# Attention and mixture-of-depths on one core: a group prepared 16 steps ahead, weights and selected rows loaded at other places in the queue

## The chip, the core and the metric

The kernel runs on one core of a Trainium2 chip. The metric is the device time of one execution in microseconds (us), where lower is better. Everything is in float32.

## The reference

Two blocks follow each other. The first is attention with normalized queries and keys, for 8 batches, 12 heads, 448 tokens and head size 64; the second routes 128 tokens of each batch through a two-layer network.

```
q_n = q / sqrt(mean(q*q) + 1e-6) * g_q           # over the head size, k_n likewise
attn = softmax(q_n @ k_n.T / sqrt(64))
x    = (attn @ v) as (8, 448, 768)
scores = x @ w_gate                               # one number per token
top    = the 128 tokens of a batch with the highest scores
out    = x, and for the tokens of top: x + sigmoid(score) * (relu(x @ w1) @ w2)
```

w1 is 768 x 1024 and w2 is 1024 x 768.

## The kernel before

**Work and its units.** The twelve heads of a batch are cut into three groups of four heads, so there are 24 groups. A group has 7 steps, one for each block of 64 keys; 168 steps in all. A step is `scores` (16 small matmuls on PE into `sc`, two exponentials of 128x448 on ACT into `p`), `values` (16 matmuls into `av`) and `add_probs` (one addition on DVE into `sum`). When the last step of a group is done, `values_out`, `sum_keys`, `invert_sums` and `to_tokens` copy, divide and transpose the result into `x`, one token per row. Three groups make a batch; `gate`, `spread`, `ranks_of`, `count` and `annotate` then find the rank of each token, `select` scatters the 128 chosen rows from `x` to DRAM (four indirect DMAs on POOL's queue), `load_selected` reads them back as `xe` on SP's queue, and `mixture` runs the two-layer network on them in pieces.

**Preparation of a group.** `prepare(n, slot)` puts six things into a table: `squares` on ACT (L193) and the reduction `sum_squares` on DVE (L199), each twice, for queries (tile 0) and keys (tile 1); the power -1/2 is on POOL (L203). Then `rows_out` (L216) writes the queries' factors to DRAM as `rows`, and `rows_in` (L228) reads them back spread over the partitions as `bc`. `scale_q` (L237, DVE) multiplies `qT` by `bc` four steps before the group's first scores. The keys' factors go into the exponential as its scale.

**Order.** The order is written by hand, and each engine executes its queue in that order. `at(slot, fn)` enters a function under a step; one pass of the main loop, here called a round, takes four steps: it emits their scores and the values of earlier ones, then runs the table's entries for its slots in two halves, and after each half a piece of the mixture, if one is running. `ready[b]` says from which round on batch b's mixture may start: the later of `now + 3` and `first_ff(b)`. All plain loads and stores are issued by SP, in order; where one has to wait for a semaphore, all behind it wait too.

Before the change, group n is prepared from step 7n - 12 on, its token tiles are loaded at 7n - 20, q at 7n - 13, k and v at 7n - 11. The first preparation of this kind, that of group 2, starts at step 4. The 14 parts of the weights (`load_w`, L181) are loaded at steps 8 to 21, with the gate's weights `wg` (L177) ahead of them. `constants` (L161 to L173), at step 9, makes a table of comparisons and the token numbers on POOL, and DVE copies the numbers to `token_f`. `load_selected` (L484) is entered three steps after the ranks' first count.

Of the kernel before, what the change touches and what calls it, by code (L numbers as in the profile page):

```python
# [10 lines left out]
F32 = mybir.dt.float32  # L11
# [6 lines left out]
def _bcast_row(ap_1d: bass.AP, parts: int) -> bass.AP:  # L18
    return dataclasses.replace(ap_1d, ap=[[0, parts]] + [list(x) for x in ap_1d.ap])
# [7 lines left out]
def fast(  # L27
# [25 lines left out]
    nc = tc.nc  # L53

    B, NP, _, S = qT.shape
    CP = 112
    NJ = S // CP
    D = 64
    NI = S // D
# [15 lines left out]
    norm_pool = ctx.enter_context(tc.tile_pool(name="norm", bufs=2))  # L75
# [65 lines left out]
    for c in range(2):  # L141
        nc.vector.memset(pick_pair[D * c : D * (c + 1), c : c + 1], 1.0)
    nc.vector.scalar_tensor_tensor(
        out=gg, in0=gcol[:, 0:1], scalar=scale, in1=gcol[:, 1:2], op0=OP.mult, op1=OP.mult
# [6 lines left out]
    wg = const.tile([CP, DM], F32, name="wg")  # L151
# [21 lines left out]
        nc.vector.tensor_copy(out=token_f, in_=token_i)  # L173

    def load_w(part):
        if part == 0:
            nc.sync.dma_start(out=wg, in_=_bcast_row(moe_w_gate, CP))  # L177
        for w, src in ((w1, moe_w1), (w2, moe_w2)):
            n = w.shape[1]
            if part < n:  # L180
                nc.sync.dma_start(  # L181
                    out=w[:, part], in_=src.rearrange("(c p) f -> p c f", p=128)[:, part]
                )
            part -= n
            if part < 0:
                return
# [3 lines left out]
    def squares(n, i):  # L190
        t = toks.pop((n, i))
        sq = norm_pool.tile([128, 2, NI, D], F32, name="sq")
        nc.scalar.activation(out=sq, in_=t, func=AF.Square, scale=scale)  # L193
        sss[n, i] = norm_pool.tile([128, 2, NI], F32, name="ss", bufs=4)
        return sq

    def sum_squares(n, i, sq):
        ss = sss.pop((n, i))
        nc.vector.tensor_reduce(out=ss, in_=sq, axis=AX.X, op=OP.add)  # L199
        nc.vector.tensor_scalar_add(out=ss, in0=ss, scalar1=1e-6)  # L200
        rinv = norm_pool.tile([128, 2, NI], F32, name="rinv", bufs=6)
        flat = "p h i -> p (h i)"
        nc.gpsimd.tensor_tensor(  # L203
            out=rinv.rearrange(flat),
            in0=ss.rearrange(flat),
            in1=neg_half.to_broadcast([128, 2 * NI]),
            op=OP.pow,
        )
        rinvs[n, i] = rinv
# [206 lines left out]
    def score_rows(b):  # L416
        t = rowss[b]
        ps = aux([128, 512], "row_ps")
        for j in range(NJ):
            nc.tensor.transpose(  # L420
                out=ps[:CP, CP * j : CP * (j + 1)], in_=t[:, j, :], identity=ident[:CP, :CP]
            )
        rows = moe_pool.tile([CP, S], F32, name="score_rows")
        nc.scalar.copy(out=rows, in_=ps[:CP, 0:S])
        rowss[b] = rows
# [153 lines left out]
    def at(slot, fn, *args):  # L579
        todo.setdefault(slot, []).append(lambda: fn(*args))  # L580
# [8 lines left out]
    def prepare(n, slot):  # L589
        sq = {}  # L590
        for i in range(2):
            at(slot + 2 * i, lambda i=i: sq.setdefault(i, squares(n, i)))
            at(slot + 2 * i + 1, lambda i=i: sum_squares(n, i, sq.pop(i)))
        at(slot + 4, rows_out, n)
        at(slot + 5, rows_in, n)

    for n in range(1, n_groups):
        s0 = NI * n
        if n > 2:
            at(s0 - 20 if n > 3 else 0, load_tok, n, 0)  # L600
            at(s0 - 20 if n > 3 else 0, load_tok, n, 1)
        at(max(s0 - 4, 3), scale_q, n)
        if n > 1:
            prepare(n, max(s0 - 12, 4))
            at(max(s0 - 13, 2), load_q, n)
            at(max(s0 - 11, 2), load_k, n)
            at(max(s0 - 11, 2), load_v, n)
    for part in range(NDC + NFC):
        at(8 + part, load_w, part)
    at(9, constants)  # L610

    def finish(n, q):

# [5 lines left out]
    now = [0]  # L619

    def last_tokens(n):
        to_tokens(n, 1)
        b, g = divmod(n, NG)
        q = now[0]

        s = PER * (q + 1) if n < n_groups - 1 else -9
        at(s, gate, n)
        if g < NG - 1:
            return
        at(s, store_x, b)  # L630
        at(s + 1, spread, b)
        task((q + 1, 1) if n < n_groups - 1 else (q + 1, 0), ranks_of, b)

    def ranks_of(b):
        score_rows(b)
        s = PER * (now[0] + 1) if b < B - 1 else -9
        at(s, count, b, (0, 1))
        at(s + 1, count, b, (2, 3))
        at(s + 2, annotate, b)
        at(s + 2, select, b)  # L640
        at(s + 3, load_selected, b)
        if b < B - 1:
            ready[b] = max(now[0] + 3, first_ff(b))
        else:
            ready[b] = 0

    def first_ff(b):


        return (units + 4 - NG * NI * (B - 2 - b)) // PER  # L650
# [15 lines left out]
    sq = {}  # L666
    sq[0, 0] = squares(0, 0)
    sum_squares(0, 0, sq.pop((0, 0)))
    sq[0, 1] = squares(0, 1)
    sum_squares(0, 1, sq.pop((0, 1)))  # L670
    sq[1, 0] = squares(1, 0)
    sq[1, 1] = squares(1, 1)
# [25 lines left out]
    moe, ready, done, q = iter(()), {}, 0, 0  # L698
# [475 lines left out]
def _build(nc, ap, cap, out):  # L1174
    D = ap["g_q"].shape[0]
    with tile.TileContext(nc) as tc:
        with tc.tile_pool(name="bound", bufs=1) as pool:
            g = pool.tile([1, 2, D], F32, name="g")
            nc.sync.dma_start(out=g[:, 0], in_=ap["g_q"].rearrange("(one d) -> one d", one=1))
            nc.sync.dma_start(out=g[:, 1], in_=ap["g_k"].rearrange("(one d) -> one d", one=1))  # L1180


            prod = pool.tile([1, D], F32, name="prod")
            nc.vector.tensor_mul(out=prod, in0=g[:, 0], in1=g[:, 1])
            nc.vector.tensor_mul(out=prod, in0=prod, in1=prod)
            top = pool.tile([1, 1], F32, name="top")
            nc.vector.tensor_reduce(out=top, in_=prod, axis=AX.X, op=OP.max)
            small = pool.tile([1, 1], I32, name="small")
            nc.vector.tensor_scalar(
                out=small,  # L1190
                in0=top,
                scalar1=MAX_SCORE * MAX_SCORE / D,
                scalar2=None,
                op0=OP.is_le,
            )
            is_small = nc.values_load(small[0:1, 0:1], min_val=0, max_val=1,
                skip_runtime_bounds_check_because="a comparison gives 0 or 1")
        with tc.If(is_small > 0) as cmp, tc.manual_schedule():  # L1198
            fast(
                tc, *(ap[n] for n in ("qT", "kT", "vp", "tok", "g2")),  # L1200
                *(ap[n] for n in _INS[5:]), cap, out,
            )
        with cmp.Else():
            general(tc, *(ap[n] for n in _INS), cap, out)
# [43 lines left out]
```

## Time and profile before

| | us |
|---|---|
| median of 3 runs (lowest, highest) | 600.18 (598.5, 601.54) |
| profiled execution | 604.69 |
| its span, first to last instruction | 603.0 |
| PE busy | 530.8 |
| DVE busy | 353.1 |
| ACT busy | 279.5 |
| POOL busy | 193.7 |

PE is TensorE, DVE VectorE, ACT ScalarE, POOL GpSimd, and SP SyncE; PEld is PE's loading of weights, SPq the issuing of DMAs on SP. A row of the timeline gives the start and the duration, the engine, the line and operation, what it writes and reads, and in brackets how long the engine had been idle and who ended that. The granted clock is the share of TensorE's 2.4 GHz that it was allowed. Line numbers are those of the kernel before.

### The profile page before, as it was taken

What the parts mean: (1) busy time and instruction counts of PE and PEld (TensorE: products, weight loads), DVE (VectorE), ACT (ScalarE), POOL (GpSimd) and SP (SyncE); (2) the same over time, 40 slices, a digit from 0 to 9 for tenths busy, and PEclk for the clock granted to TensorE, in tenths of its full rate; (3) what the DMA queues carried; (4) which work ended last, traced back from release to release, by engine and by line L of the source; (5) the groups of instructions that cost most, each with busy time, mean ns of one, the idle gap of its engine ahead of it and who ended that gap; (6) DMA issues with size and microseconds to landing.
All of it is one profiled execution on the core that took longest, in us unless ns stands there. A gap on an engine that the chain in (4) does not pass through costs nothing. (4 is left out here: it accounts for less than half of the span.)

```text
span 603.0 us, 16322 instructions
## 1 busy us (share of the span) xinstructions
PE 530.8 (88%) x7028; PEld 294.3 (49%) x7028; DVE 353.1 (59%) x699; ACT 279.5 (46%) x506; POOL 193.7 (32%) x100
## 2 busy tenths in 40 slices
PE   6793887799999799996999999999998999937995
PEld 6330323236645366442665466446643664417683
DVE  2363776966575947483557766857573856453100
ACT  3571666555645445544454546444644644511010
POOL 3352333543132623053225432535052620130200
PEclk9986988899999799997999999999999999977999
DMA  6559775765805267507534626283806521013200
GB/s 234 198 163 335 224 268 196 238 206 186 276 21 193 58 212 245 185 9 251 207 119 137 228 75 244 60 272 118 277 8 201 180 80 46 27 30 112 58 28 30
DMA packets 47108, 94.02 MB, mean 156 GB/s; under 512 B 11702, under 2 KB 29878, under 8 KB 47028
## 3 DMA queue, kind: packets, MB, share of 16 engines
q1 hardware_dynamic: 43684, 86.58, 42.8%
q0 software_dynamic: 3200, 6.31, 3.2%
q8 instruction: 57, 0.93, 0.6%
q14 instruction: 23, 0.19, 0.1%
q10 hardware_dynamic: 144, 0.00, 0.0%
HBM read 75.39 MB, written 25.36 MB: 167 GB/s over the span
## 5 line engine op out<-in xcount | busy, mean ns | idle before, releaser
L287 ACT ACTIVATE p<-sc,rinv 128x448 f32<-128x448 f32 x336 | 187.1, 638 | 123.7 <-PE sc L278 73.2
L203 POOL TENSOR_TENSOR rinv<-ss,neg_half 128x14 f32<-128x14 f32 x48 | 139.2, 2905 | 297.0 <-DVE ss L200 197.1
L278 PE MATMUL sc<-qT,kT 64*32 64x448 f32 x2688 | 164.7, 569 | 31.7 <-issue 21.5
L304 PE MATMUL av<-p,v 64*32 64x448 f32 x2688 | 160.9, 556 | 0.3 <-issue 0.2
L317 DVE TENSOR_TENSOR sum<-sum,p 128x896 f32<-128x896 f32 x120 | 130.5, 1088 | 31.7 <-ACT p L287 25.3
L278 PEld LDWEIGHTS sc<-qT,kT 64*32 64x32 f32 x2688 | 51.0, 109 | 107.2 <-issue 74.2
L304 PEld LDWEIGHTS av<-p,v 64*32 64x32 f32 x2688 | 60.9, 112 | 81.6 <-issue 74.5
L524 PE MATMUL moe_ps<-xeT,w 128*128 128x128 f32 x672 | 80.8, 278 | 0.0
L524 PEld LDWEIGHTS moe_ps<-xeT,w 128*128 128x128 f32 x672 | 78.1, 194 | 2.9 <-issue 2.9
L543 PE MATMUL moe_ps<-w,hT 128*128 128x384 f32 x224 | 77.6, 491 | 1.4 <-DVE xe L552 0.7
L373 DVE TENSOR_TENSOR x<-x_ps,rden 112x512 f32<-112x512 f32 x48 | 32.9, 688 | 44.1 <-PE x_ps L371 44.1
L199 DVE TENSOR_REDUCE ss<-sq 128x14 f32<-128x896 f32 x48 | 51.6, 1075 | 11.7 <-ACT sq L193 11.7
L543 PEld LDWEIGHTS moe_ps<-w,hT 128*128 128x128 f32 x224 | 40.5, 190 | 28.6 <-issue 2.2
L466 POOL DMA_INDIRECT selected<-x,rank x32 | 39.0, 1217 | 42.0 <-DVE x L458 34.2
L237 DVE SCALAR_TENSOR_TENSOR qT<-qT,gg,bc 128x896 f32<-128x896 f32 x23 | 26.1, 1136 | 41.7 <-DMA bc<-rows 41.7
L193 ACT ACTIVATE sq<-tok 128x896 f32<-128x896 f32 x48 | 45.6, 963 | 5.6 <-DMA tok<-in_tok_dram 5.6
L397 DVE SCALAR_TENSOR_TENSOR prod<-x,wg 112x256 f32<-112x256 f32 x96 | 40.5, 422 | 2.5
L533 ACT ACTIVATE hT<-moe_ps 128x512 f32<-128x512 f32 x14 | 8.4, 597 | 58.2 <-PE moe_ps L524 58.2
L371 PE MATMUL x_ps<-ident,xT 128*112 128x128 f32 x192 | 29.1, 281 | 3.6 <-ACT xeT L505 3.0
L561 POOL DMA_INDIRECT out_dram<-xe,row x8 | 11.0, 1374 | 61.4 <-DVE rden L359 29.5
L371 PEld LDWEIGHTS x_ps<-ident,xT 128*112 128x112 f32 x192 | 21.3, 135 | 18.1 <-issue 9.7
L317 DVE TENSOR_TENSOR sum<-p 128x896 f32<-128x896 f32 x24 | 25.8, 1076 | 6.5 <-ACT p L287 6.5
(63 smaller groups left out, 243.6 us busy)
## 6 DMA issues: line engine op xcount, KB each, us to landing
tok<-in_tok_dram SPq DMA_DIRECT2D x48, 448.0 KB, 6.9
qT<-in_qT_dram SPq DMA_DIRECT2D x24, 448.0 KB, 6.0
kT<-in_kT_dram SPq DMA_DIRECT2D x24, 448.0 KB, 7.5
v<-in_vp_dram SPq DMA_DIRECT2D x24, 448.0 KB, 7.9
out_dram<-x SPq DMA_DIRECT2D x8, 1344.0 KB, 7.1
bc<-rows SPq DMA_DIRECT2D x46, 224.0 KB, 3.8
xe<-selected SPq DMA_DIRECT2D x8, 385.0 KB, 3.2
w<-in_moe_w_dram SPq DMA_DIRECT2D x6, 512.0 KB, 10.2
```

The costliest lines, as they stand in the source:

```text
L193: nc.scalar.activation(out=sq, in_=t, func=AF.Square, scale=scale)
L199: nc.vector.tensor_reduce(out=ss, in_=sq, axis=AX.X, op=OP.add)
L203: nc.gpsimd.tensor_tensor(out=rinv.rearrange(flat), in0=ss.rearrange(flat), in1=neg_half.to_broadcast([128, 2 * NI]), op=OP.pow,)
L278: nc.tensor.matmul(out=scs[hh][o : o + 32, 0:S], lhsT=kTs[n][r, c, D * i + k0 : D * i + k0 + 32], rhs=qTs[n][r, c, :], start=True, stop=True,)
L287: nc.scalar.activation(out=p[:, hh], in_=scs[hh][:, 0:S], func=AF.Exp, scale=rinvs[n, 1][:, hh, i : i + 1],)
L304: nc.tensor.matmul(out=avs[n][c][o : o + 32, 0:S], lhsT=vs[n][r, hh, i, d0 : d0 + 32], rhs=probs[u][r, hh], start=(i == 0), stop=(i == NI ...
L317: nc.vector.tensor_tensor(out=sums[n], in0=probs[u - 1] if i == 1 else sums[n], in1=probs[u], op=OP.add)
L371: nc.tensor.transpose(out=ps[:CP, j, :], in_=t[:, j, :], identity=ident)
L397: nc.vector.scalar_tensor_tensor(out=prod, in0=xs[b][:, j, cols], scalar=1.0, in1=wg[:, cols], op0=OP.mult, op1=OP.mult, accum_out=gates[b ...
L466: w = nc.gpsimd.indirect_dma_start(out=t[:, :], out_offset=bass.IndirectOffsetOnAxis(ap=rank[:, j : j + 1], axis=0), in_=x[:, j, :], in_of ...
L524: nc.tensor.matmul(out=ps[:, 128 * i : 128 * i + n], lhsT=w1[:, dc, 128 * (f0 + i) : 128 * (f0 + i + 1)], rhs=xeT[:, dc, :n], start=(dc == 0),
L543: nc.tensor.matmul(out=ps[:n, : DM // 2], lhsT=hT[:, fc, :n], rhs=w2[:, fc, cols], start=(fc == 0), stop=(fc == NFC - 1),)
```

## The change

Groups from 2 on are prepared four steps earlier, and `rows_in` comes two steps after `rows_out` instead of one; token tiles are loaded 24 instead of 20 steps ahead. `wg` is loaded at step 7 and the weights at every second step from 18 to 44; the constants move to step 18. `load_selected` comes four steps later, except in the last batch, and a mixture may start at `now + 4`. The ring of `rinv` tiles grows from 6 to 8.

```diff
-        if part == 0:
-            nc.sync.dma_start(out=wg, in_=_bcast_row(moe_w_gate, CP))
...
-        rinv = norm_pool.tile([128, 2, NI], F32, name="rinv", bufs=6)
+        rinv = norm_pool.tile([128, 2, NI], F32, name="rinv", bufs=8)
...
         at(slot + 4, rows_out, n)
-        at(slot + 5, rows_in, n)
+        at(slot + 6, rows_in, n)
...
         if n > 2:
-            at(s0 - 20 if n > 3 else 0, load_tok, n, 0)
-            at(s0 - 20 if n > 3 else 0, load_tok, n, 1)
+            at(max(s0 - 24, 0), load_tok, n, 0)
+            at(max(s0 - 24, 0), load_tok, n, 1)
         at(max(s0 - 4, 3), scale_q, n)
         if n > 1:
-            prepare(n, max(s0 - 12, 4))
+            prepare(n, max(s0 - 16, 0))
...
     for part in range(NDC + NFC):
-        at(8 + part, load_w, part)
-    at(9, constants)
+        at(18 + 2 * part, load_w, part)
+    at(7, lambda: nc.sync.dma_start(out=wg, in_=_bcast_row(moe_w_gate, CP)))
+    at(18, constants)
...
-        at(s + 3, load_selected, b)
+        at(s + 7 if b < B - 1 else s + 3, load_selected, b)
         if b < B - 1:
-            ready[b] = max(now[0] + 3, first_ff(b))
+            ready[b] = max(now[0] + 4, first_ff(b))
```

What this does to the queues is seen best in three places. The first is SP's queue from the loads of group 2's k and v on, before (`rows` and `bc` are those of group 2):

```order
L100 DMA kT<-in_kT_dram 128x2x448
L100 DMA v<-in_vp_dram 128x896
L216 DMA rows<-rinv 64x2x7 x2
L100 DMA qT<-in_qT_dram 128x2x448
L100 DMA tok<-in_tok_dram 128x896 x2
L177 DMA wg<-in_moe_w_gate_dram 112x768
L181 DMA w_210<-in_moe_w_dram 128x1024
L228 DMA bc<-rows 64x2x448 x2
```

and after the change:

```order
L100 DMA kT<-in_kT_dram 128x2x448
L100 DMA v<-in_vp_dram 128x896
L214 DMA rows<-rinv 64x2x7 x2
L100 DMA tok<-in_tok_dram 128x896 x2
L226 DMA bc<-rows 64x2x448 x2
L608 DMA wg<-in_moe_w_gate_dram 112x768
```

Between `rows` and `bc` of group 2 there are now only two token tiles; `wg` follows `bc`, and no weight is near.

The second is SP's queue around the load of batch 2's selected rows (`xe`), before (the `rows` and the `bc` beside it are those of group 13):

```order
L100 DMA v<-in_vp_dram 128x896
L216 DMA rows<-rinv 64x2x7 x2
L484 DMA xe<-selected 128x770
L228 DMA bc<-rows 64x2x448 x2
L100 DMA qT<-in_qT_dram 128x2x448
```

and after the change (the first `bc` is that of group 13, and `rows` are those of group 14):

```order
L226 DMA bc<-rows 64x2x448 x2
L100 DMA tok<-in_tok_dram 128x896 x2
L100 DMA qT<-in_qT_dram 128x2x448
L214 DMA rows<-rinv 64x2x7 x2
L100 DMA kT<-in_kT_dram 128x2x448
L100 DMA v<-in_vp_dram 128x896
L482 DMA xe<-selected 128x770
L226 DMA bc<-rows 64x2x448 x2
```

The load has moved behind that `bc` and behind the next group's `rows`, k and v. In batch 5 it is the same, with group 21.

The third is PE's queue at the end, from the last values on, before (`den_ps` and `denT_ps` invert the last group's sums, `x_ps` are its transposes, L500 transposes `xe` of batch 6, L524 is the first layer, `row_ps` ranks batch 7):

```order
L304 MATMUL av<-p,v 32x448 x16
L339 MATMUL den_ps<-sum,pick_pair 32x224 x4
L357 MATMUL denT_ps<-ident,den 112x128 x2
L500 MATMUL moe_ps<-ident,xe 128x128 x3
L500 MATMUL xeT_ps<-ident,xe 128x128 x3
L371 MATMUL x_ps<-ident,xT 112x128 x4
L524 MATMUL moe_ps<-xeT,w_210 128x128 x12
L371 MATMUL x_ps<-ident,xT 112x128 x4
L524 MATMUL moe_ps<-xeT,w_210 128x128 x12
L420 MATMUL row_ps<-ident,spread 112x112 x4
```

and after the change:

```order
L302 MATMUL av<-p,v 32x448 x16
L337 MATMUL den_ps<-sum,pick_pair 32x224 x4
L355 MATMUL denT_ps<-ident,den 112x128 x2
L369 MATMUL x_ps<-ident,xT 112x128 x8
L498 MATMUL moe_ps<-ident,xe 128x128 x3
L498 MATMUL xeT_ps<-ident,xe 128x128 x3
L522 MATMUL moe_ps<-xeT,w_210 128x128 x24
L418 MATMUL row_ps<-ident,spread 112x112 x4
```

The eight transposes of `x` have moved ahead of those that read `xe`.

## Rows read from the trace of the kernel before

**Rows 1.** The page's head: the span.
```profile
span 603.0 us, 16322 instructions
```
**Rows 2.** Stages: start:end, length, busy PE, PEld, DVE, ACT, POOL, clock, DMA, GB/s.
```profile
30.00:62.00 32.00, 20.10 (x314) 7.21 (x314) 17.22 (x21) 14.57 (x25) 12.75 (x9) 0.79 0.73 238
62.00:134.00 72.00, 59.42 (x979) 24.54 (x972) 53.65 (x98) 44.46 (x80) 29.47 (x12) 0.91 0.69 230
```
**Rows 3.** Timeline of PE, 44 to 66 us: start, duration, work, [idle before <- releaser].
```profile
44.41 1.71 PE L304 MATMUL av<-p,v 64*32 64x448 f32 x32
56.52 3.24 PE L278 MATMUL sc<-qT,kT 64*32 64x448 f32 x32 [10.40 <-issue]
59.48 2.66 PE L304 MATMUL av<-p,v 64*32 64x448 f32 x32
...
64.02 1.74 PE L278 MATMUL sc<-qT,kT 64*32 64x448 f32 x32
```
**Rows 4.** Timeline of DVE, 29 to 56 us.
```profile
29.75 1.15 DVE L237 SCALAR_TENSOR_TENSOR qT<-qT,gg,bc 128x896 f32<-128x896 f32 x1 [8.65 <-DMA bc<-rows]
...
35.40 1.08 DVE L199 TENSOR_REDUCE ss<-sq 128x14 f32<-128x896 f32 x1
...
46.24 0.17 DVE L173 CAST token_f<-token_i 112x4 f32<-112x4 int32 x1 [5.16 <-POOL token_i L172]
55.27 1.15 DVE L237 SCALAR_TENSOR_TENSOR qT<-qT,gg,bc 128x896 f32<-128x896 f32 x1 [8.85 <-DMA bc<-rows]
```
**Rows 5.** Timeline of SP's issues, 28 to 47 us.
```profile
28.67 0.65 SPq L100 DMA_DIRECT2D v<-in_vp_dram  x1
39.38 1.25 SPq L216 DMA_DIRECT2D rows<-rinv  x2
...
42.47 2.07 SPq L177 DMA_DIRECT2D wg<-in_moe_w_gate_dram  x1
...
45.40 1.25 SPq L228 DMA_DIRECT2D bc<-rows  x2
```
**Rows 6.** DMA issues of the whole span: count, KB each, median us to landing.
```profile
bc<-rows SPq DMA_DIRECT2D x46, 224.0 KB, 3.8
...
w<-in_moe_w_dram SPq DMA_DIRECT2D x6, 512.0 KB, 10.2
```
**Rows 7.** Timeline of PE around 283 and 465 us.
```profile
282.33 1.75 PE L278 MATMUL sc<-qT,kT 64*32 64x448 f32 x16 [4.87 <-issue]
283.80 3.13 PE L304 MATMUL av<-p,v 64*32 64x448 f32 x32
...
465.27 0.99 PE L278 MATMUL sc<-qT,kT 64*32 64x448 f32 x16 [2.13 <-ACT p L287]
```
**Rows 8.** Timeline of DVE at the same two places.
```profile
281.08 1.15 DVE L237 SCALAR_TENSOR_TENSOR qT<-qT,gg,bc 128x896 f32<-128x896 f32 x1 [9.57 <-DMA bc<-rows]
...
464.02 1.15 DVE L237 SCALAR_TENSOR_TENSOR qT<-qT,gg,bc 128x896 f32<-128x896 f32 x1 [10.03 <-DMA bc<-rows]
```
**Rows 9.** Timeline of SP's issues, 263 to 277 us.
```profile
263.43 1.96 SPq L216 DMA_DIRECT2D rows<-rinv  x2
275.25 0.33 SPq L484 DMA_DIRECT2D xe<-selected  x1
275.75 1.24 SPq L228 DMA_DIRECT2D bc<-rows  x2
```
**Rows 10.** Timeline of PE at the end, 544 to 552 us.
```profile
544.54 0.87 PE L500 MATMUL moe_ps<-ident,xe 128*128 128x128 f32 x3 [6.31 <-DMA xe<-selected]
...
546.63 1.10 PE L371 MATMUL x_ps<-ident,xT 128*112 128x128 f32 x4 [0.57 <-ACT xeT L505]
...
551.15 0.60 PE L371 MATMUL x_ps<-ident,xT 128*112 128x128 f32 x4
```
**Rows 11.** Timeline of PE at 80 and at 117 us.
```profile
80.64 0.58 PE L339 MATMUL den_ps<-sum,pick_pair 128*32 128x224 f32 x8 [2.12 <-DVE sum L317]
...
117.18 3.76 PE L278 MATMUL sc<-qT,kT 64*32 64x448 f32 x32 [3.27 <-ACT p L287]
```

## The prediction

> **What bounds the kernel now.** I began with the span and the busy time by stage. The profiled execution took 604.69 us around a span of 603.0 [rows 1], 4.5 above the median of the three runs, 600.18; my sum is made against the former and its difference is taken off the latter. In the stretch 30 to 62 us PE is busy for only 20.10 of 32 us and at 0.79 of its clock, in 62 to 134 for 59.42 of 72 at 0.91 [rows 2]. No other engine is fuller there: DVE has 17.22 and 53.65. So early on something makes all of them wait.
>
> Next, PE in order of time around the largest gap. It stops at 46.12 and starts the scores of step 14 (the first of group 2) at 56.52, after 10.40 idle. The wait costs twice: behind it the scores of two steps take 3.24 where 1.74 is usual, and the values 2.66 where 1.71 is usual [rows 3]. TensorE came out of the idle time at the lower of its two levels, 1.2 instead of 2.4 GHz; the 0.79 of this stretch mixes both [rows 2]. DVE says who is late: it waits until 55.27 for `bc` of group 2 [rows 4]. SP says why: `rows` go out at 39.38, then q, two token tiles, `wg` (2.07 to issue) and a weight are issued, and only at 45.40 `bc`, which lands almost 10 us later [rows 5]; the usual `bc` takes 3.8 [rows 6].
>
> The same picture returns twice, from another cause. At 282.33 PE has been idle for 4.87 and its values then take 3.13; at 465.27 it has been idle for 2.13 [rows 7]. Both times DVE had waited about 10 us for `bc` [rows 8]. Here SP stood at the load of the selected rows: `rows` issued at 263.43, then nothing until `xe` at 275.25, and `bc` right behind it at 275.75 [rows 9].
>
> The end is a chain: PE waits 6.31 for the selected rows of batch 6, and the last eight transposes of `x` stand behind that wait, although they need nothing from it [rows 10].
>
> **The change, part by part.** No arithmetic is added or removed; what counts is the order in each queue.
>
> 1. *Group 2 is prepared in round 0, weights later.* Its first reduction moves ahead of the wait of 8.65 that DVE has until 29.75 [rows 4], so it starts between 21.1 (29.75 − 8.65) and 28.6. Before, `rows` were issued 4.0 after this reduction started (35.40 to 39.38), which gives 25 to 32.6; SP is free at 29.3, behind the load of v [rows 5]. Before, `bc` followed 6.0 later (39.38 to 45.40): now 35.3 to 38.6. With a landing between 3.8 [rows 6] and the 9.9 seen here, `bc` is there at 39 to 48.5. DVE ended its work at 41.08 (46.24 − 5.16, [rows 4]), now with one reduction more at 42.2; PE arrives at 46.12. Only with the latest `bc` and a scaling of 1.15 does PE still wait, up to 3.5. I take no wait, since both token and weight traffic now stand behind this `bc`. Gain: 10.40 + (3.24 − 1.74) + (2.66 − 1.71) = **12.9**, at least 9.3.
>
> 2. *The load of selected rows moves four steps.* Before, it stood between `rows` and `bc` of one group, and SP waited there for the scatters. Now that `bc` is issued first. When SP then comes to the load, it has just waited for `rows` of the next group, whose power on POOL stands behind the four scatters in POOL's queue, so little is left to wait for; behind it stands the next group's `bc`, which is not due for six steps. Gains: 4.87 + (3.13 − 1.71) = **6.3** at 282 and **2.1** at 465 [rows 7]. If only `bc` comes in time, but another wait (below) takes its place, half of that remains. The load itself has at least a round and a half to the mixture that reads it; the only wait of PE for it is the one at the end [rows 10]. It costs nothing as long as this lead lasts; without it PE would wait as there.
>
> 3. *The mixture may start a round later* (now + 4). By the program's own arithmetic this delays batches 1, 2 and 6 by one round; for the others the second bound is later anyway. At the end this puts the transposes of the last `x` into PE's wait of 6.31: 1.10 + 0.60 = **1.7** less behind it [rows 10]. For batch 1 it makes three rounds in a row without matmuls of a mixture, where PE is fast and DVE must keep up. Such stretches hold the wait of 3.27 at 117.18 [rows 11]; the cost lies between 0 and one more wait of that kind, 3.3. I take the middle, **−1.6**, since the later batches get a mixture round in exchange.
>
> 4. *Reductions leave round 4.* At 80.64 PE waits 2.12 for a sum that stands on DVE behind two reductions of group 4 [rows 11], 2 × 1.08 [rows 4]. These now run in round 3: **2.1**, at least 0.
>
> 5. *The constants move to step 18.* DVE waited 5.16 for POOL's `token_i`, inside the great wait, so it cost nothing [rows 4]. That cover is gone, and behind DVE's copy stand the products that free PE's auxiliary bank. It can cost 0 to 5.16; POOL can do them beside DVE's sums, gate and scaling of that round, so I take **−1.0**, near the lower end.
>
> 6. The two added `rinv` buffers, `wg` apart from the weights and the loads of q, k, v are covered by SP's free time and cost nothing; should SP be late, the first to wait would be `bc` of groups 4 to 8.
>
> Sum: 12.9 + 6.3 + 2.1 + 1.7 + 2.1 − 1.6 − 1.0 = 22.5. The profiled execution would take 582.2, the median 577.7; I say **577.5**. The bounds: with 9.3 for part 1, 3.2 for half of the 282 wait, 1.0 for half of the other, 1.7, 0, −3.3 and −5.2 only 6.7 is left (593); all at their best give 25.1 (575).
>
> What I leave where it is: the wait of 3.27 at 117.18 with the slow 3.76 behind it [rows 11], in which ACT holds exponentials behind the gate of a batch. DVE's work before that gate is nearly the same in the new order.
>
> **The rivals.**
> *The gain is half given back.* With the great wait gone, DVE has no idle stretch to catch up in, and each round without a mixture is decided by it: 53.65 of 72 busy, in bursts [rows 2]. For it: the waits of [rows 11] are DVE's. Against it: DVE was idle in the same 10 us and is moved ahead with PE. Price: half of parts 1 and 2, 10.6, which gives 588.
>
> *More than the sum.* The stretch 62 to 134 tightens as well, since `bc` and reductions are ready ahead: PE's own idle time there is 72 − 59.42 = 12.6 [rows 2]. All of it would give 565. Against: the waits left there lie in one batch's chain, which doesn't move. The Trainium skill, "Perfetto Trace Analysis", section "Identifying the Most-Contended Engine", says that matmul busy time is a poor measure of PE's limit, whereas occupancy is fair for VectorE. By that rule DVE's 53.65 would be the limit and 18.4 could go, which would give 559; no row shows this stretch at such a density.
>
> *Slower: weights in the way of `bc`.* The 14 weight loads now lie between steps 18 and 44, between the `bc` of groups 4 to 8, on the same queue. If these land as late as that of group 2 did, each costs up to 12.9. It decides when `bc` comes later than its scaling by more than its lead, which is six steps now, about one and a half rounds of some 10 us, against one step before. Two such waits cancel the gain; three give 577.5 + 38.6 = 616. The Trainium skill, "DMA: Bandwidth & Descriptors", section "Queues, rings and completion order", says that each DMA engine takes the descriptors of a queue row in order and that SP owns a single row. By that rule a `bc` behind weights waits for them all, and the trace agrees: 9.9 against 3.8. A weight of 512 KB lands in 10.2 [rows 6], which is less than the lead, and that speaks against it.
>
> *The change doesn't do what it says.* `bc` stays late, because SP still stands at another wait ahead of it; then only the end and little else is gained, some 2: 598.
>
> **How the numbers follow.** The forecast, with its own bounds, 0.57; half given back 0.22; more than the sum 0.12; slower 0.04; no effect 0.05. The range of 565 to 591 takes in the forecast almost to its worst bound, the half and part of the greater gain. A measurement of this kernel can tell about 0.5%, 3 us, from no change, so faster means below 597.2. The first three cases lie below it: 0.91; same 0.05; slower 0.04.
>
> **What would show it.** Right: PE runs through 46 to 56 with scores of two steps at 1.7; of DVE's waits for `bc` the one at 29.75 stays, those of 55.27, 281.08 and 464.02 go; SP's standing at `xe` shrinks to a few us; the last eight transposes precede the selected rows of batch 6. Part 3 would be wrong if PE waits grow in rounds 15 to 17, part 5 if DVE waits over 1 us for `token_i`. The whole is wrong if DVE still waits for `bc` of groups 4 to 8, or if the stretch from 62 to 134 is as long as before after it began 12 us earlier.

## The result and the profile after

The changed kernel took 572.03 us (median of 4 runs, 571.14 to 573.61) beside 599.66 for the kernel before (598.5 to 601.54): a ratio of 0.9539 with an interval of 0.9506 to 0.9573, or 25.6 to 29.6 us less. 577.5 was forecast, a gain of 22.5 where the medians show 27.6. So it went the way and nearly the size that was forecast; not every term did.

First the page of the changed kernel: span, busy times, and the landing of `bc` (columns of the last: transfer, queue, operation, count, size of one, median us to landing).

```profile
span 570.4 us, 16312 instructions
...
PE 515.3 (90%) x7028; PEld 288.5 (51%) x7028; DVE 354.7 (62%) x699; ACT 278.3 (49%) x506; POOL 196.6 (34%) x100
...
bc<-rows SPq DMA_DIRECT2D x46, 224.0 KB, 5.9
```

`bc` lands in 5.9 in the median instead of 3.8 [rows 6]. The stages of [rows 2] again:

```profile
30.00:62.00 32.00, 29.29 (x492) 11.73 (x500) 27.07 (x40) 22.05 (x39) 18.70 (x8) 0.90 0.73 232
62.00:134.00 72.00, 61.55 (x1026) 28.38 (x1018) 54.42 (x100) 43.28 (x79) 33.39 (x16) 0.95 0.90 292
```

PE is now busy for 29.29 of 32 us in the first stretch, and the granted clock is 0.90. The DMA share of the second has grown: all 14 weight loads are issued from 61.67 on now, before it was nine of them from 62 on.

The `den_ps` row of a group (the sums of its keys, once a group) serves as a calendar, numbered 0 to 23 here. PE's timeline of the changed kernel, with the rows of groups 0, 1, 3, 4, 11, 15, 19 and 20 and the places that the prediction named:

```profile
42.16 0.59 PE L337 MATMUL den_ps<-sum,pick_pair 128*32 128x224 f32 x8
...
46.63 1.71 PE L276 MATMUL sc<-qT,kT 64*32 64x448 f32 x32
...
51.21 0.59 PE L337 MATMUL den_ps<-sum,pick_pair 128*32 128x224 f32 x8 [0.35 <-DVE x L371]
...
67.53 0.58 PE L337 MATMUL den_ps<-sum,pick_pair 128*32 128x224 f32 x8 [0.99 <-DVE sum L315]
...
97.91 0.59 PE L337 MATMUL den_ps<-sum,pick_pair 128*32 128x224 f32 x8
...
103.05 2.53 PE L276 MATMUL sc<-qT,kT 64*32 64x448 f32 x29 [1.22 <-ACT p L285]
...
115.40 0.58 PE L337 MATMUL den_ps<-sum,pick_pair 128*32 128x224 f32 x8
...
185.47 3.32 PE L276 MATMUL sc<-qT,kT 64*32 64x448 f32 x32 [4.33 <-ACT p L285]
...
253.03 0.59 PE L337 MATMUL den_ps<-sum,pick_pair 128*32 128x224 f32 x8
...
344.81 0.59 PE L337 MATMUL den_ps<-sum,pick_pair 128*32 128x224 f32 x8
...
427.35 0.59 PE L337 MATMUL den_ps<-sum,pick_pair 128*32 128x224 f32 x8
...
446.23 0.59 PE L337 MATMUL den_ps<-sum,pick_pair 128*32 128x224 f32 x8 [0.62 <-ACT xeT L503]
...
507.30 1.91 PE L369 MATMUL x_ps<-ident,xT 128*112 128x128 f32 x8
514.26 0.88 PE L498 MATMUL moe_ps<-ident,xe 128*128 128x128 f32 x3 [5.04 <-DMA xe<-selected]
```

The kernel before was profiled once more (it closes the experiments). That execution had a span of 596.1, nearer to the usual, and the gains are read against it. Its PE, the same eight groups, with the wait in batch 2:

```profile
41.23 0.58 PE L339 MATMUL den_ps<-sum,pick_pair 128*32 128x224 f32 x8
...
63.21 0.58 PE L339 MATMUL den_ps<-sum,pick_pair 128*32 128x224 f32 x8 [0.35 <-DVE x L373]
...
109.70 0.58 PE L339 MATMUL den_ps<-sum,pick_pair 128*32 128x224 f32 x8
...
130.93 0.58 PE L339 MATMUL den_ps<-sum,pick_pair 128*32 128x224 f32 x8
...
266.89 0.58 PE L339 MATMUL den_ps<-sum,pick_pair 128*32 128x224 f32 x8
...
279.10 1.75 PE L278 MATMUL sc<-qT,kT 64*32 64x448 f32 x16 [7.71 <-issue]
...
365.16 0.58 PE L339 MATMUL den_ps<-sum,pick_pair 128*32 128x224 f32 x8
...
448.57 0.58 PE L339 MATMUL den_ps<-sum,pick_pair 128*32 128x224 f32 x8
...
470.06 0.59 PE L339 MATMUL den_ps<-sum,pick_pair 128*32 128x224 f32 x8 [0.62 <-ACT xeT L505]
```

The gain by place, each the time between two such rows before minus the time between them after, for the first two 63.21 − 41.23 = 21.98 against 51.21 − 42.16 = 9.05:

| stretch | gain | forecast |
|---|---|---|
| start to group 0 | −0.9 | 0 |
| group 0 to 1: preparation of group 2 | 12.9 | 12.9 (part 1) |
| group 1 to 3: round 4, constants | −0.2 | 1.1 (parts 4, 5: 2.1 − 1.0) |
| group 3 to 4: gate of batch 0 | 3.7 | 0 |
| group 4 to 11: gate and mixture of batch 1 | −1.7 | −1.6 (part 3) |
| group 11 to 15: batch 2 | 6.5 | 6.3 (part 2) |
| group 15 to 19 | 0.9 | 0 |
| group 19 to 20: batch 5 | 2.6 | 2.1 (part 2) |
| group 20 to the end | 1.9 | 1.7 (part 3) |
| sum | 25.7 | 22.5 |

Group 0's row lies between 41.23 and 43.17 in all the traces of this case, whatever the kernel, so the −0.9 of the first line is no more than scatter. Read against the first profile of before, whose differences the prediction had used, the gate of batch 0 comes to 5.0, group 4 to 11 to 0.0, batch 2 to 8.0 and group 15 to 19 to 3.2, in a sum of 32.6; so between two executions of one kernel a line of this table moves by up to 2.3.

The terms look well met, save for the gate of batch 0. The experiments show that not all of them are met for the reason given.

DVE after, at the places of [rows 4], then at its copy of the token numbers and at the scaling of group 5:

```profile
29.07 1.15 DVE L235 SCALAR_TENSOR_TENSOR qT<-qT,gg,bc 128x896 f32<-128x896 f32 x1 [5.10 <-DMA bc<-rows]
...
41.47 1.15 DVE L235 SCALAR_TENSOR_TENSOR qT<-qT,gg,bc 128x896 f32<-128x896 f32 x1
...
63.32 0.17 DVE L173 CAST token_f<-token_i 112x4 f32<-112x4 int32 x1 [1.03 <-POOL token_i L172]
...
88.16 1.15 DVE L235 SCALAR_TENSOR_TENSOR qT<-qT,gg,bc 128x896 f32<-128x896 f32 x1
```

Of the waits for `bc` only the first, 5.10, is left. SP after, at `bc` of group 2 and at batch 2:

```profile
35.41 1.82 SPq L226 DMA_DIRECT2D bc<-rows  x2
...
253.80 1.25 SPq L214 DMA_DIRECT2D rows<-rinv  x2
...
257.96 0.38 SPq L482 DMA_DIRECT2D xe<-selected  x1
258.62 1.26 SPq L226 DMA_DIRECT2D bc<-rows  x2
```

`bc` of group 2 went out at 35.41, inside the forecast 35.3 to 38.6; it was 45.40 before [rows 5]. At the selected rows SP no longer stands: 257.96, behind `rows` and the loads of k and v, and `bc` of group 14 right behind it. The standing has moved ahead of these `rows`: SP issues nothing from 235.7 to 253.80, until POOL has come through the four scatters (from 244.88) to the power behind them (250.88). `bc` of group 13 had gone out ahead of that, at 229.20.

### The profile page after: what moved, and what is told of

The parts are those of the page before. It is cut to its first block, busy times and chain, and to the rows that moved or that the text cites. A ratio compares the mean times of both kernels' runs of the same rounds, so it can differ in the third digit from the quotient of the medians.

```text
span 570.4 us, 16312 instructions
## 1 busy us (share of the span) xinstructions
PE 515.3 (90%) x7028; PEld 288.5 (51%) x7028; DVE 354.7 (62%) x699; ACT 278.3 (49%) x506; POOL 196.6 (34%) x100
## 5 line engine op out<-in xcount | busy, mean ns | idle before, releaser
L201 POOL TENSOR_TENSOR rinv<-ss,neg_half 128x14 f32<-128x14 f32 x48 | 142.9, 2981 | 218.3 <-issue 102.8
L276 PE MATMUL sc<-qT,kT 64*32 64x448 f32 x2688 | 155.4, 553 | 13.4 <-ACT p L285 7.1
L302 PE MATMUL av<-p,v 64*32 64x448 f32 x2688 | 151.6, 547 | 0.0
L302 PEld LDWEIGHTS av<-p,v 64*32 64x32 f32 x2688 | 56.4, 109 | 74.3 <-issue 67.1
L276 PEld LDWEIGHTS sc<-qT,kT 64*32 64x32 f32 x2688 | 49.2, 108 | 85.8 <-issue 54.1
L464 POOL DMA_INDIRECT selected<-x,rank x32 | 36.0, 1125 | 64.6 <-DVE x L456 56.7
L559 POOL DMA_INDIRECT out_dram<-xe,row x8 | 12.3, 1533 | 82.0 <-DVE rden L357 46.4
L357 DVE RECIPROCAL rden<-denT_ps 112x16 f32<-112x16 f32 x24 | 6.1, 254 | 40.1 <-PE denT_ps L355 40.0
L550 DVE SCALAR_TENSOR_TENSOR xe<-moe_ps,xe 128x384 f32<-128x384 f32 x14 | 8.6, 616 | 35.6 <-PE moe_ps L541 35.6
```

The costliest lines, as they stand in the source:

```text
L201: nc.gpsimd.tensor_tensor(out=rinv.rearrange(flat), in0=ss.rearrange(flat), in1=neg_half.to_broadcast([128, 2 * NI]), op=OP.pow,)
L276: nc.tensor.matmul(out=scs[hh][o : o + 32, 0:S], lhsT=kTs[n][r, c, D * i + k0 : D * i + k0 + 32], rhs=qTs[n][r, c, :], start=True, stop=True,)
L302: nc.tensor.matmul(out=avs[n][c][o : o + 32, 0:S], lhsT=vs[n][r, hh, i, d0 : d0 + 32], rhs=probs[u][r, hh], start=(i == 0), stop=(i == NI ...
L464: w = nc.gpsimd.indirect_dma_start(out=t[:, :], out_offset=bass.IndirectOffsetOnAxis(ap=rank[:, j : j + 1], axis=0), in_=x[:, j, :], in_of ...
```

## Experiments

In this section "the changed kernel" is the one of the diff above.

**1. The preparation alone**, put into the kernel before:

```diff
-prepare(n, max(s0 - 12, 4))
+prepare(n, max(s0 - 16, 0))
...
-at(slot + 5, rows_in, n)
+at(slot + 6, rows_in, n)
```

The token tiles 24 steps ahead and the eight buffers of `rinv` go with it.

> The kernel before with the preparation alone moved: 16 steps ahead, token tiles 24 steps ahead, bc two steps behind rows, 8 rinv tiles. Theory 'each wait has its own edit': only the great wait at group 2 and the reductions of group 4 go, 13 to 15 us faster, and the waits at batches 2 and 5 stay. Rival 'the lead covers all': with six steps between bc and its use, SP's standing at the load of selected rows hides as well, 24 to 27 us faster.

575.31 us, ratio 0.9591 (0.9548 to 0.9635): 25 less, as the rival had it. The waits at 282 and 465 are gone although the load of selected rows is issued at its old step. In batch 2 SP stands at it for 20.7 us (239.49 to 260.23), longer than before; but `bc` of group 13 has gone out ahead of it, at 237.13, and the next one, at 268.16, is not wanted before 281.04. SP there:

```profile
237.13 1.25 SPq L228 DMA_DIRECT2D bc<-rows  x2
...
260.23 0.33 SPq L484 DMA_DIRECT2D xe<-selected  x1
```

So the preparation alone brings `bc` past the load, and the load's move is not needed for it. Group 2 gains only part: DVE and PE there,

```profile
48.58 0.17 DVE L173 CAST token_f<-token_i 112x4 f32<-112x4 int32 x1 [6.58 <-POOL token_i L172]
```

```profile
49.91 3.21 PE L278 MATMUL sc<-qT,kT 64*32 64x448 f32 x32 [3.07 <-issue]
```

DVE waits 6.58 for GpSimd's `token_i` just ahead of the scaling of group 2, and PE stands 3.07 until that is done. It is not a wait for `bc`: the constants at step 9 now lie where the great wait used to cover them.

**2. Weights, gate row and constants alone**, put into the kernel before.

```diff
-        if part == 0:
-            nc.sync.dma_start(out=wg, in_=_bcast_row(moe_w_gate, CP))
...
-    at(8 + part, load_w, part)
-at(9, constants)
+    at(18 + 2 * part, load_w, part)
+at(7, lambda: nc.sync.dma_start(out=wg, in_=_bcast_row(moe_w_gate, CP)))
+at(18, constants)
```

> The kernel before with the weights, wg and the constants alone moved. Theory 'bc of group 2 is late because of the weights ahead of it on the queue': 6 to 10 us faster, since rows are still written late and bc still has one step of lead. Rival 'it is late because it is prepared late': at most 3 us faster.

607.07 us, ratio 1.0135 (1.0091 to 1.0179): 1.4% slower, where both the theory and the rival had it faster. PE's wait at group 2 shrinks from 10.40 to 7.24 only. DVE, then PE:

```profile
79.09 0.17 DVE L173 CAST token_f<-token_i 112x4 f32<-112x4 int32 x1 [6.06 <-POOL token_i L172]
...
149.75 1.15 DVE L235 SCALAR_TENSOR_TENSOR qT<-qT,gg,bc 128x896 f32<-128x896 f32 x1 [6.84 <-DMA bc<-rows]
```

```profile
84.43 0.97 PE L337 MATMUL den_ps<-sum,pick_pair 128*32 128x224 f32 x8 [8.35 <-DVE sum L315]
...
152.82 0.97 PE L337 MATMUL den_ps<-sum,pick_pair 128*32 128x224 f32 x8 [5.41 <-DVE x L371]
```

Two new waits appear. The constants stand behind a power on POOL (72.58 to 75.1), and DVE waits for them. And `bc` of group 7 comes 6.84 late: its `rows` are issued at 135.53 behind three weights, and `bc` only at 143.94, 8.4 later; in experiment 12 this takes 4.7 (131.48 to 136.18). That is nearly the mechanism of the rival "weights in the way of `bc`", though what the weights hold up here is the write of `rows` ahead of it (`bc` itself lands in 3.8 in the median, as before); it needs no more than the short lead.

**3. The load and the later mixture alone**, put into the kernel before.

```diff
-at(s + 3, load_selected, b)
+at(s + 7 if b < B - 1 else s + 3, load_selected, b)
...
-ready[b] = max(now[0] + 3, first_ff(b))
+ready[b] = max(now[0] + 4, first_ff(b))
```

> The kernel before with the load of selected rows four steps later and the mixture at now + 4 alone. Theory: the waits at batches 2 and 5 and the transposes at the end go, 8 to 9 us faster by the sum (6.3 + 2.1 + 1.7 - 1.6), and up to 14 if all of the 10 us gained around batch 2 belong to this edit. Rival 'the lead decides, not the place of the load': under 4 us, little more than the 1.7 at the end.

585.22 us, ratio 0.9776 (0.9734 to 0.9818), 15 us less, more than either theory or rival had said. The waits at 282 and 465 go here too, while PE's 9.72 at group 2 stays. Preparation and load are two cures for the same waits; their gains, 25 and 15, do not add.

**4. The changed kernel with load and round undone** (the diff of 3 the other way round).

> The changed kernel with the load of selected rows and the mixture's start as before. Theory 'each wait has its own edit': 8 to 14 us slower than the changed kernel, some 580 to 586. Rival 'the lead covers all': 1 to 3 us slower than the changed kernel, some 573 to 575, with only the end longer.

569.10 us, ratio 0.9504 (0.9461 to 0.9547): not slower, against theory and rival alike. The interval overlaps that of the changed kernel, so the times alone don't say faster, but the traces say where they part. Up to group 8 they agree to 0.3 us; at group 15 the changed kernel is at 344.81, this one at 340.31. The stretch from group 8 to group 15, of the changed kernel and of this one (columns: stretch, its length, then busy time and count of PE, PEld, DVE, ACT and POOL, granted clock, DMA share, GB/s):

```profile
191.61:344.81 153.20, 146.47 (x2051) 84.79 (x2044) 103.34 (x199) 80.86 (x147) 56.19 (x26) 1.00 0.62 187
```

```profile
191.38:340.31 148.93, 145.18 (x2051) 84.34 (x2044) 103.53 (x199) 80.42 (x147) 56.06 (x26) 1.00 0.64 191
```

With a granted clock of 1.00 in both, PE's idle time is 153.20 − 146.47 = 6.7 against 148.93 − 145.18 = 3.8, and its work takes 1.3 longer. The extra idle time is in PE's waits of 1.76, 0.90 and 1.52 for DVE (225.94, 243.50 and 272.81). At the same three operations experiment 4, whose mixture is further on there, has no wait (226.01, 242.64 and 277.19); why DVE is later in the changed kernel was not tested. From group 11 to 15 this kernel gains 365.16 − 340.31 − (266.89 − 251.93) = 9.9 on the kernel before, the changed one 6.5.

**5. The round alone undone.**

```diff
-ready[b] = max(now[0] + 4, first_ff(b))
+ready[b] = max(now[0] + 3, first_ff(b))
```

> The changed kernel with the mixture of batches 1, 2 and 6 allowed three rounds after the ranks again instead of four; the selected rows stay four steps later. Theory A (the fourth round is what cost: it pushes mixture work into rounds 19 to 23, where the changed kernel lost 4.5 us against the kernel that has the load and the round undone): the 4.5 us come back, the end loses the 1.8 us of transposes that ran ahead there, 569 to 570 us. Theory B (the later load itself costs, since the mixture now waits for rows that land later): 572 us or more, and a new wait of PE for the transfer of xe stands at the start of a mixture.

580.67 us, ratio 0.9686 (0.9659 to 0.9714). I expected a gain of 2 to 3; it lost 8.6, and theory B held. PE:

```profile
203.01 0.55 PE L498 MATMUL moe_ps<-ident,xe 128*128 128x128 f32 x3 [3.71 <-DMA xe<-selected]
...
270.27 0.90 PE L498 MATMUL moe_ps<-ident,xe 128*128 128x128 f32 x3 [5.20 <-DMA xe<-selected]
```

The mixtures of batches 1 and 2 now stand 3.71 and 5.20 at the selected rows, and from group 2 to group 12 the kernel loses 11.9 to experiment 4. The later load needs the later round: "it costs nothing as long as this lead lasts" was the condition, and the fourth round is what keeps it.

**6. Later load and fourth round for batch 6 alone.**

```diff
-at(s + 7 if b < B - 1 else s + 3, load_selected, b)
+at(s + 7 if b == B - 2 else s + 3, load_selected, b)
...
-ready[b] = max(now[0] + 4, first_ff(b))
+ready[b] = max(now[0] + (4 if b == B - 2 else 3), first_ff(b))
```

> The changed kernel with the later load and the fourth round kept for batch 6 alone; all other batches as before the change. Theory: the two effects are separable, so the 4.5 us of rounds 19 to 23 come back and the 1.8 us of transposes ahead of the tail stay: 567 to 568 us. Rival: the tail's gain needs the displaced mixture work of the rounds before it, and the end is that of the kernel with load and round undone, 569 to 570 us; or the loss of rounds 19 to 23 comes from something else and it is 571 to 572 us.

567.95 us, ratio 0.9466 (0.9434 to 0.9499). The interval lies below that of the changed kernel, so this version beats it. From experiment 4 it can't be told apart: the intervals overlap, and its profiled span is 568.3 against 567.6 there. Its last eight transposes precede the selected rows, as in the changed kernel; from group 23 to the end it takes 66.3, against 66.8 in experiment 4 and 65.1 in the changed kernel, so of the 1.7 at the end only 0.5 is there.

**7. Weights, gate row and constants undone in the changed kernel (both pairs of lines), and 8. the constants alone (the second pair).** `wg` goes back into `load_w` in experiment 7.

```diff
-    at(18 + 2 * part, load_w, part)
+    at(8 + part, load_w, part)
...
-at(18, constants)
+at(9, constants)
```

> The changed kernel with the weights from step 8 on, the gate's row at the first of them and the constants at step 9, as before the change. Theory (preparation and late weights are both needed for group 2's 13 us, for the preparation alone gave 7.5 of them): 5 to 6 us slower than the changed kernel, 577 to 578 us; PE waits about 3 us near 50, and DVE's wait for a broadcast near 29.5 is above 5 us. Rival (once the preparation stands in front of them, the weights cost nothing wherever they stand): 571 to 573 us.

> The changed kernel with the constants at step 9 again; the weights stay late. Theory (what the kernel with weights and constants undone lost at group 2 is DVE's 6.58 us wait for GpSimd's token numbers at 48.11, and not the weights): the same 577 to 578 us, with that DVE wait of 6 to 7 us near 48 and a PE wait of 3 us near 49. Rival (the weights ahead of the broadcast rows cost it): 571 to 573 us, no PE wait over 2 us near 49.

577.78 us, ratio 0.9652 (0.9625 to 0.9678), and 577.25, ratio 0.9660 (0.9614 to 0.9706). The two agree, so with the early preparation, and the constants at step 9 in both, the place of the weights costs nothing that these times show; and constants at step 9 cost 5.2 by the medians (4.1 by the spans, 574.5 in experiment 8 against 570.4). At step 8 the weights stand behind `bc` of group 2 too: it is issued at 35.53 in experiment 7, the first weight at 38.55. In experiment 8 DVE's wait at 48.93 is the 6.58 of experiment 1 again, and PE stands 3.89 behind it.

**9. Only group 2 early.** The kernel of experiment 4, with every later group prepared twelve steps ahead as before.

```diff
-prepare(n, max(s0 - 16, 0))
+prepare(n, 0 if n == 2 else s0 - 12)
```

Token tiles and `rows_in` of the later groups are as before the change.

> The kernel with the load and the fourth round undone (569.1 us), with only group 2 prepared at step 0; every later group is prepared twelve steps ahead as before the change, its tokens and broadcast rows too. Weights and constants late. Theory (the lead of the later groups is what takes away the waits at 282 and 465 and DVE's wait ahead of the gate of batch 0): the 13 us at group 2 stay, and the 5.0 us at the gate of batch 0, about 10 us before batch 2's end and 2 us before batch 6's come back: 584 to 587 us. Rival (the whole gain hangs on the start: once group 2 is early everything behind it is): 569 to 572 us.

598.57 us, ratio 1.0012 (0.9979 to 1.0045): nothing is left of the gain, and more than expected was lost. The 13 us at group 2 are there (group 1 at 52.22). Then DVE, and PE:

```profile
70.27 0.17 DVE L173 CAST token_f<-token_i 112x4 f32<-112x4 int32 x1 [6.08 <-POOL token_i L172]
...
141.93 1.15 DVE L235 SCALAR_TENSOR_TENSOR qT<-qT,gg,bc 128x896 f32<-128x896 f32 x1 [7.37 <-DMA bc<-rows]
```

```profile
145.00 0.97 PE L337 MATMUL den_ps<-sum,pick_pair 128*32 128x224 f32 x8 [5.94 <-DVE x L371]
...
281.02 1.75 PE L276 MATMUL sc<-qT,kT 64*32 64x448 f32 x16 [8.55 <-issue]
```

The old wait in batch 2 is back (8.55), and with it the two of experiment 2: 6.08 for the constants, 7.37 for a `bc` whose `rows` went out behind weights. The later places of weights and constants do little harm with a lead of sixteen steps and cost much with twelve, so this run doesn't price the lead alone.

**10. The gate two steps later.**

```diff
-at(s + 2, annotate, b)
-at(s + 2, select, b)
+at(s + 4 if b < B - 1 else s + 2, annotate, b)
+at(s + 4 if b < B - 1 else s + 2, select, b)
```

> The changed kernel with the gate's exponential and the indirect writes two steps later for every batch but the last. Theory: what is left at the gate of batch 1 (PE waits 4.33 us at 185.47, behind an exponential that ACT gives out while the counts on DVE are not done) goes, because ACT can run exponentials of the scores while DVE counts: 3 to 6 us less, 566 to 569 us, and no PE wait above 1 us within 180 to 190. Rival: DVE, not the order on ACT, is late there, and the wait moves two steps on with its size: 571 to 573 us.

573.43 us, ratio 0.9577 (0.9547 to 0.9608): no gain. PE's 4.33 at 185.47 becomes 2.98 at 193.00, two steps on: group 8 comes 5.3 earlier, and by group 9 4.9 of it is given back. ACT's exponential of the gate still waits for DVE, 3.28 instead of 5.14. So the rival held in the main: the wait moves on with most of its size. Not all of it: from group 7 to group 9 this kernel is 1.4 shorter. But its end, from group 23 on, takes 69.1 against 65.1, since PE waits 7.45 for the selected rows of batch 6, which are written later (5.04 in the changed kernel). With batch 6 left as it was, it was not run.

**11. DVE's copy of the token numbers six steps after POOL's part**, in the kernel of experiment 6.

```diff
-        nc.vector.tensor_copy(out=token_f, in_=token_i)
...
+at(24, lambda: nc.vector.tensor_copy(out=token_f, in_=token_i))
```

> The kernel with later load and fourth round for batch 6 alone (567.95 us), and DVE's conversion of the token numbers six steps behind GpSimd's making of them. Theory: DVE no longer stands 1.04 us at 63.08, PE's wait of 1.00 us at 67.28 goes, and 1 us less: 566 to 568 us, a difference that the times alone can hardly tell but the trace can. Rival: another product ends last at 67 and nothing changes.

568.41 us, ratio 0.9497 (0.9451 to 0.9543): nothing. The wait of 1.00 ahead of group 2's sums goes; behind it PE's wait for ACT's copy `den` grows to 2.23 from 1.22.

**12. The kernel before, profiled again.**

> The kernel before, unchanged, profiled a second time: its first profiled execution took 604.69 us, 5 us more than the median of its runs, and the gains by place were read against it. Theory (the 5 us are spread over the waits at 282, 465 and the gates, which come out a little differently each time): a span of 597 to 600 us, with the same waits and 3 to 5 us less between 270 and 290. Rival (the first profile is typical of every profiled execution): a span of 602 to 604 us and the same numbers to 0.5 us.

597.91 us, span 596.1. The waits stand at the same places; what differs is how the lost time shows. In batch 2 DVE waits 9.55 for `bc`, as in the first profile (9.57, [rows 8]); but PE stands 7.71 here and stood 4.87 there [rows 7], since it had come later to the same wait (the 16 values at 272.51 had taken 2.92). The other differences lie at the gates of batches 0 and 1 (1.3 and 1.4) and between groups 12 and 16 (3.4). Of the 32.6 us between the first profiles some 7 are thus the first one's own.

## Why the prediction was right, and where it was not

*What bounds the kernel.* Right. All three great waits were `bc` that came late, and the earlier preparation cures them all but for the 3.07 that the constants cause (experiment 1). Without it for the later groups, and with weights and constants late, the whole gain is gone (experiment 9).

*Part 1, group 2.* 12.9 forecast, 12.9 measured. The reason given was "since both token and weight traffic now stand behind this `bc`". For the tokens it is wrong: the order of SP's queue has two token tiles ahead of it (issued at 30.12, `bc` at 35.41), and it came in time all the same. For the weights it is true, but the preparation does it and not the part's "weights later": at their old steps they stand behind it as well (experiment 7). What the early preparation needs beside it is that the constants leave step 9.

*Part 5, constants.* The wait left behind is as forecast: 1.03 on DVE at 63.32, about 1 at PE. The error was to price the move by that alone. Staying at step 9 costs some 5 (experiment 8), which the forecast had inside part 1 without knowing it.

*Part 2, the load of selected rows.* The sum was met, 6.5 and 2.6 against 6.3 and 2.1, and the attribution failed. SP's queue did what part 2 said, and without the preparation load and round together are worth 15 us (experiment 3). Given the preparation the move gains nothing (experiment 4; the waits are gone in experiment 1 as well). So that the sum was met is luck, for two errors of size cancelled: the wait in batch 2 was worth 9.9, since PE's own 4.87 understated it, and load and round together took 3.4 back.

*Part 3, the later mixture.* The end is right (1.9 for 1.7). −1.6 was taken for rounds 15 to 17, and the table's −1.7 looks like it, but half of that is batch 1's gate, whose wait grew from 3.38 to 4.33. The prediction had named such a growth as a sign against part 3; it is not part 3's, for experiment 4, without it, has the same wait (4.34). Beside experiment 4, which starts 0.2 earlier, the changed kernel is 1.1 late at group 11 and 4.5 at group 15, so load and round together cost 4.3 there, 2.7 more than the term, and this falls mostly on batch 2. The exchange that the later batches were to get didn't come: the 4.5 stay until the last group. Still the round is needed once the load is moved (experiment 5).

*Part 4, reductions.* The wait at 80.64 fell from 2.12 [rows 11] to 0.99 at 67.53, and what is left is part 5's wait: net 1.1, as forecast. But by group 3 it is given back, to PE's wait for `den` right behind (1.23 at 69.34, 0.47 before) and the one for the gate's `spread` (2.89 at 88.30, 2.20 before). Experiment 11 shows the same sliding.

*What was left where it is: this step failed.* "DVE's work before that gate is nearly the same" is true of the work, not of a wait ahead of it. DVE in the first profile of before:

```profile
105.28 1.15 DVE L237 SCALAR_TENSOR_TENSOR qT<-qT,gg,bc 128x896 f32<-128x896 f32 x1 [3.75 <-DMA bc<-rows]
...
112.07 0.68 DVE L433 SCALAR_TENSOR_TENSOR cmp<-score_rows,gate,earlier 112x448 f32<-112x448 f32 x1
```

Ahead of the counts that the gate waits for (from 112.07 on) DVE had stood 3.75 for `bc` of group 5. After, that scaling runs at 88.16 without a wait, and PE's 3.27 with its slow 3.76 [rows 11] becomes 1.22 with 2.53. The stretch gives 3.7 against the second profile, where DVE's wait is 3.40 and PE's 2.94. That is 3.7 of the missing 5; the table's sum stops at 25.7, and the rest up to the medians' 27.6 lies within their interval. The experiments agree: where this wait of DVE is left (2: 2.97, 3: 3.51, 9: 2.96), PE stands 2.50, 3.17 and 2.48 at the gate, and where it is gone (1 and 4) 1.22. A reduction that stood between the counts has moved behind them with it, which no run separates. At the gate of batch 1 DVE had stood only 0.83 for `bc` (at 183.00 in the first profile), and PE's wait stayed (4.33 at 185.47).

*The rivals.* "Weights in the way of `bc`" did not come: `bc` lands later (5.9 against 3.8), but within its lead. It is 7.9 between 60 and 110 us, where weights stand, but also 6.2 between 200 and 400, where none do: `bc` now follows right behind k and v. The Trainium skill, "DMA: Bandwidth & Descriptors", section "Queues, rings and completion order", has each DMA engine take the descriptors of a queue row in order, and that longer landing agrees. With the short lead something like it came twice (experiments 2 and 9), at 5.41 and 5.94 of PE, not 12.9. Of "half given back" came 4.3, the cost of load and round, where 10.6 was priced. "More than the sum" came in part: its reason, that `bc` is ready ahead, is what freed the gate of batch 0 (with the reduction that no run separates), and its "the waits left there lie in one batch's chain, which doesn't move" was wrong. But PE's idle time between 62 and 134 us is still 72 − 61.55 = 10.5, where 12.6 was the price of all of it.

## What to carry to other kernels

A wait in one queue can be cured where it arises (the load moved) or where it hurts (a longer lead). Here the second cure covers all such waits, and the first, with the later round that it needs, adds a cost, so try them singly before keeping both. When a great wait goes, list what ran in its shadow, a small copy behind another engine's work above all, and move that with it. Price a stall by a whole stretch between two fixed rows: neither PE's gap nor the wait of the engine that needs the data is its worth. In batch 2 PE's 4.87 and DVE's 9.57 stood for 9.9, in batch 5 PE's 2.13 and DVE's 10.03 for 2.6. And look for the same late transfer ahead of every other gate.

## What was not expected of the hardware

GpSimd's instructions of one form have more than one duration. In experiment 1, while DVE stands, the power, the filling and the four selects take

```profile
42.08 2.58 POOL L203 TENSOR_TENSOR rinv<-ss,neg_half 128x14 f32<-128x14 f32 x1 [1.06 <-DVE ss L200]
44.61 1.59 POOL L161 MEMSET earlier<- 112x1792 f32 x1
46.27 2.18 POOL L163 TENSOR_SCALAR_AFFINE_SELECT earlier<-earlier 112x448 f32<-112x448 f32 x4
```

and in the changed kernel, with DVE at work,

```profile
41.64 3.42 POOL L201 TENSOR_TENSOR rinv<-ss,neg_half 128x14 f32<-128x14 f32 x1 [1.06 <-DVE ss L198]
...
58.41 1.60 POOL L161 MEMSET earlier<- 112x1792 f32 x1
60.09 3.10 POOL L163 TENSOR_SCALAR_AFFINE_SELECT earlier<-earlier 112x448 f32<-112x448 f32 x4
```

that is 2.58 against 3.42 and 2.18 against 3.10, while the filling, which reads nothing, stays at 1.6. The short selects lie inside a wait of DVE before the change and in experiments 1, 2, 7, 8 and 9; what makes the others longer was not tested by itself. The Trainium skill, "SBUF — State Buffer", section "SBUF: two separate sides", says that a GpSimd operation that reads SBUF and a VectorE operation with two inputs there exclude each other; these rows fit that. In these rows a small operation on GpSimd is thus longer just when DVE is at work.
